# A decay-attention and snake-MLP kernel: head tables and casts placed anew, and the second and third chunks' scores and state products moved among the projection matmuls

## Chip, cores, metric

One core of one Trainium2 chip runs the whole program. The metric is device time of one launch in microseconds (us). The time before is the median of three runs, 211.49 us (210.94 to 211.74).

The engines are TensorE (PE; its weight loads are shown as PEld), VectorE (DVE), ScalarE (ACT), GpSimd (POOL) and SyncE (SP). Each runs its own instructions strictly in the order in which the program lists them, and waits on semaphores for what other engines and transfers deliver. So where an instruction stands in its engine's list decides what is queued behind it while it waits.

## What is computed

Attention with a decay per head over blocks, then an MLP with a snake activation:

```python
# q, k, v: [4, 8, 768, 64]; lam: [8], 0.97 to 0.99
for b in range(nb):                       # blocks along the sequence
    intra = einsum('bhic,bhjc->bhij', qb, kb) * Dmask     # lam**(i-j), i >= j
    intra = einsum('bhij,bhjd->bhid', intra, vb)
    inter = einsum('bhid,bhde->bhie', qb * lam_pow, kv_state)
    out = intra + inter
    kv_state = lam_block * kv_state + einsum('bhsd,bhse->bhde', kb * rev_pow, vb)
x = out.transpose(0, 2, 1, 3).reshape(3072, 512)
h = x @ w_in                              # [3072, 2048]
s = sin(alpha * h)
g = h + s * s / (alpha + 1e-9)
y = g @ w_out                             # [3072, 512], float32
```

## The kernel before

The sequence of 768 is cut into six chunks of 128 rows, t = 0 to 5. A chunk of all four batches gives 512 rows of x; the MLP on them is group g = t. While group g runs through the MLP, the attention of chunk g+1 is slotted between its matmuls. Nothing schedules this: the order of every engine is that in which the source emits it.

Attention of one chunk. k and q are turned (transposed) so that heads lie on partitions, by TensorE and a copy (`turn`, `turns_pair`) or by a transposing transfer (`turn_by_dma`). `scores` are the products of k and q. `masks` multiply them on VectorE with the decay mask. `states` are the products of decayed k (`kdec`, made by GpSimd in `decay_k`) and v. `update` adds them on VectorE to the decayed state and has GpSimd cast the new state (`cast_state`). `outputs_first` multiplies q with the state, `outputs` adds the masked scores times v in the same PSUM bank, and `leave` moves that with the row decay to `xt`, the MLP's input. Chunk 0 has no state yet and uses one block of 128: `scores1`, `outs`, `states1`, with the mask table C0. Its k and q are handled batch by batch; batch 0 and k of batch 1 come as float32 and are cast on VectorE. `spin` issues matmuls of no use that fill TensorE's time in the head.

MLP of one group. `hidden(g, f)` is four matmuls for one of 16 feature tiles f, a sine on ScalarE, and a square, on ScalarE or for some f of group 0 on VectorE (`squarer`). `finish` makes the gated value `gall` on VectorE from square, `r_sb` = 1/alpha and the PSUM bank. `project(g, m, part)` is four matmuls with a quarter of w_out (one unit); after part 3 `store` evicts the row m. Units of group g wait in a list, and `run(n)` takes the next n of it: most of group 0's between and after its own hidden tiles, the rest in group 1.

There are eight PSUM banks, named by number in the source. A bank is written again only when its last reader is done; the hidden tiles of group 0 go through `H0 = (0,1,2,3,5,6,7,4,0,1,3,5,0,1,5,0)`. GpSimd issues all loads after the first three (`load`, `load_w_in`, `load_w_out`), in its own order with its products. SyncE issues the transposing transfers and the stores.

The places that the change touches: the decay tables (L182 to 190); `squarer` (L442) and `store` (L485); the head, L516 to 565; the order after group 0's last hidden tile, L627 to 659; and the tables of what goes before and behind each f of group 1 (`slots`, `feed`, `own`, `units`, L662 to 707).

Of the kernel before, what the change touches and what calls it, by code (L numbers as in the profile page):

```python
# [8 lines left out]
ALU = mybir.AluOpType  # L9
# [6 lines left out]
def kernel(  # L16
# [11 lines left out]
    nc = tc.nc  # L28
# [153 lines left out]
    def decay_tables():  # L182
        nc.scalar.copy(out=lnlam[:, H:H + 2], in_=lnlam[:, 0:2])
        later["R128"] = powers("R128", 2, lnlam[:], [P, H + 2])
        later["NE64"] = powers("NE64", 3, lnlam[:].rearrange("p (hp hd) -> p hd hp", hd=2), [P, 2, HE])
        later["R64"] = powers("R64", 4, lnlam[:], [P, H + 2])
        for pr in range(2):
            for hd, half in enumerate(HALF):
                nc.scalar.activation(out=L64[half, pr, :], in_=lnlam[half, pr + hd:pr + hd + H - 1:2],
                                     func=ACTF.Exp, scale=float(D))  # L190
# [251 lines left out]
    def squarer(g, f):  # L442
        if g == 0:
            return V if f in (3, 5, 7, 9, 11) else A
        return A
# [39 lines left out]
    def store(g, m):  # L485
        o_sb = outp.tile([P, DM], FP32, name="o_sb")
        if g < NT - 2 and (g or m < 2):
            nc.vector.tensor_copy(out=o_sb[:], in_=ops_of.pop((g, m))[:])  # L488
        else:
            nc.scalar.copy(out=o_sb[:], in_=ops_of.pop((g, m))[:])  # L490
        held.append((m * S + g * T, o_sb))
        if g:
            put_held()
# [6 lines left out]
    def project_halves(g, m):  # L500
        for n in range(2):
            cols = slice(n * DM // 2, (n + 1) * DM // 2)
            ps = bank("hps", HB[n])
            for f in range(NFC):
# [13 lines left out]
                            in1=Rq[:].unsqueeze(2).broadcast_to([P, H, D]))  # L518
    nc.vector.tensor_copy(out=kn[0][:, 1, :, :], in_=raw["k1"][:])
    nc.vector.tensor_tensor(out=C0[:], in0=tri[:].unsqueeze(1).unsqueeze(1).broadcast_to([P, 2, HP, T]),  # L520
                            in1=NE[:].unsqueeze(3).broadcast_to([P, 2, HP, T]), op=ALU.mult)
    turn(0, "k", 0, 4, A)
    spin(2, 3)
    turn(0, "q", 0, 5, A)
    spin(2, 3)
    turn(0, "k", 1, 1, A)
    spin(3, 3)
    scores1(0, 0, (6, 7))
    turn(0, "q", 1, 2, A)
    spin(2, 3)  # L530
    nc.sync.dma_start(out=alpha_fp[:], in_=moe_alpha.rearrange("(f p) -> f p", p=P))
    turn(0, "k", 2, 0, A)
    spin(2, 3)
    scores1(0, 1, (4, 5))
    turn(0, "q", 2, 1, A)
    etab(0, 1)
    spin(3, 3)
    turn(0, "k", 3, 2, V)
    scores1(0, 2, (6, 7))
    spin(2, 3)  # L540
    turn(0, "q", 3, 0, A)
    etab(2, 3)
    decay_tables()
    spin(2, 3)
    a_ps = bank("a_ps", OB)
# [3 lines left out]
    nc.vector.tensor_copy(out=alpha_sb[:], in_=a_ps[:, 0:NFC])  # L549
    nc.vector.reciprocal(out=r_sb[:], in_=alpha_sb[:])  # L550
    spin(2, 1)
    scores1(0, 3, (4, 5))
    spin(2, 1)
    outs(0, 0, 3, A)
    outs(0, 1, 1)
# [4 lines left out]
    spin(3, 6)  # L560
    outs(0, 3, 0)
    spin(4, 6)
# [35 lines left out]
    for f in range(NFC):  # L598
        hidden(0, f)
        if f in (1, 10):  # L600
            states1(0, f // 10, 2 if f == 10 else 4)
        if f == 10:
            decay_k(1, 0, 2)
            decay_state(1, 0)
            cast_state(1, 0, home(1, 0))
            load_w_out(2)
            load(1, "q", 2, 4)
            load_w_out(3)
            load(2, "v", 0, 2)
        if f in (11, 12):  # L610
            run(1)
        if f == 12:
            turns_pair(1, "k", 0, 4, (A, A))
        if f == 13:
            turn(1, "q", 0, 2, A)
            turn(1, "q", 1, 3, V)
        if f == 14:
            scores(1, (0,), (4, 2))
            masks(1, 0)
        if f == 15:  # L620
            run(1)
            states(1, (0,), (3, 4))
            finish(0, 14)
            update(1, 0, 0)
        if f != 14:
            finish(0, f)
# [14 lines left out]
    run(3)  # L641
# [8 lines left out]
    run(1)  # L650
# [3 lines left out]
    run(1)  # L654
    outputs(1, (1,))
    leave(1, 1)
    run(1)
    decay_state(1, 0)
# [3 lines left out]
    def slots(g):  # L662
        t = g + 1
        d = {i: [] for i in range(NFC)}
        if g == 1:
            at = dict(KV=6, F=9, O=12)
        else:
            at = dict(KV=4, F=8, O=12)
        d[at["KV"]] += [(states, t)]
        for n in range(4):  # L670
            d[at["KV"] + ((0, 0, 1, 2)[n] if g == 1 else n)] += [(update, t, n // 2, n % 2)]
        d[at["F"]] += [(scores, t), (masks, t, 0)]
        d[at["F"] + 1] += [(masks, t, 1)]
        d[at["O"]] += [(outputs, t), (leave, t, 0)]
        d[at["O"] + (g > 1)] += [(leave, t, 1)]
        return d

    def feed(g):
        t = g + 1
        d = {i: [] for i in range(NFC)}  # L680
        if g == 1:
            d[2] += [(turn_by_dma, 2, 0, "k"), (pair_ready, 2, 1), (decay_state, 1, 1), (turn_by_dma, 2, 1, "k"), (turn_by_dma, 2, 0, "q")]
            d[7] += [(put_held,)]
            d[8] += [(turns_pair, 2, "q", 2, AB[0], (A, A))]
        if t + 1 < NT:
            if g == 1:
                d[7] += [(new_chunk, 3)] + [(load, 3, nm, b, b + 2) for nm, b in (("v", 0), ("k", 0), ("v", 2))]
                d[8] += [(load, 3, nm, b, b + 2) for nm, b in (("k", 2), ("q", 0), ("q", 2))]
# [10 lines left out]
    for g in range(1, NT + 1):  # L699
# [6 lines left out]
        own = {5: (0, 0), 8: (0, 1), 13: (0, 2)} if g == 1 else {}  # L706
        units = [1, 3, 5, 8, 13] if g == 1 else [i for i in range(NFC) if g > 2 or i not in (0, 1, 3)]
# [49 lines left out]
```

## Time and profile before

| | us |
|---|---|
| median of three runs | 211.49 |
| the profiled execution | 210.82 |
| its span on the core | 209.0 |
| TensorE busy | 201.0 |
| ScalarE busy | 143.1 |
| VectorE busy | 132.9 |
| GpSimd busy | 107.0 |

The span is the time from the first to the last instruction that the profiler saw; the difference to the execution's time lies around it. Busy time is what the profile shows of an engine's instructions. Matmuls are pipelined and overlap, so that TensorE's busy time is no measure of its rate. Single waits are read from the timeline, and which of them counts is read from the chain of waits, which follows the end of the program back from each step to what released it.

### The profile page before, as it was taken

How to read it: one execution, taken by the hardware profiler on the slowest of the kernel's cores; microseconds unless marked ns; L12 is line 12 of the kernel's file. 1: busy time of each engine (PE TensorE's matmuls, PEld its weight loads, DVE VectorE, ACT ScalarE, POOL GpSimd, SP SyncE). 2: the span in 40 equal slices, each digit the busy share in tenths (PEclk: the TensorE clock that was granted, in tenths of full speed). 3: DMA queues.
4: the chain of work that ended last, by engine and by line, in shares of the span. 5: the costliest groups of instructions: out<-in, count | busy, mean ns of one | idle time of the engine just before them, and what ended most of it. 6: DMA issues, size and time to landing. Idle time of an engine off the chain costs nothing.

```text
span 209.0 us, 5363 instructions
## 1 busy us (share of the span) xinstructions
PE 201.0 (96%) x2243; PEld 98.7 (47%) x2243; DVE 132.9 (64%) x218; ACT 143.1 (68%) x239; POOL 107.0 (51%) x111
## 2 busy tenths in 40 slices
PE   7999998999998999999999999999999999999993
PEld 2664444544453544445444444445444444444452
DVE  6794999473778868968547968556868544444000
ACT  4788989213999699765776775776675787887121
POOL 8989939979939993999986850002000000000000
PEclk9999999999999999999999999999999999999998
DMA  7999999999997999699999998701101101110212
GB/s 140 156 170 207 207 159 178 185 179 135 127 311 50 145 127 161 99 175 161 106 150 145 209 103 130 174 0 53 50 3 53 50 0 50 55 50 0 100 59 93
DMA packets 98794, 24.60 MB, mean 118 GB/s; under 512 B 90946, under 2 KB 95826, under 8 KB 98770
## 3 DMA queue, kind: packets, MB, share of 16 engines
q0 software_dynamic: 76176, 13.24, 86.7%
q1 hardware_dynamic: 20512, 10.50, 24.4%
q10 hardware_dynamic: 2082, 0.52, 1.4%
q8 instruction: 17, 0.28, 0.5%
q14 instruction: 7, 0.06, 0.1%
HBM read 27.27 MB, written 6.29 MB: 161 GB/s over the span
## 4 chain that ended last, share of the span: by engine, by line
PE 80%; DVE 11%; ACT 4%; DMA 2%; issue 1%; ACTq 0%
PE ops L481 37%; PE hps L453 33%; DVE gall L470 4%; DMA raw_k<-in_k_dram 2%; PE O_ps L403 2%; ACT s_sb L456 2%; ACT s L461 2%; PE hps L505 2%; DVE s L469 2%; DVE STm L304 2%; PE KV_ps L369 2%; PE O_ps L428 1%; PE F_ps L389 1%; DVE STm L396 1%; DVE xt L316 1%
## 5 line engine op out<-in xcount | busy, mean ns | idle before, releaser
L470 DVE SCALAR_TENSOR_TENSOR gall<-s,r_sb,hps 128x512 bf16<-128x512 bf16 x96 | 71.2, 745 | 45.0 <-ACT s L461 44.8
L453 PE MATMUL hps<-xt,w_in 128*128 128x512 bf16 x384 | 95.7, 379 | 1.2 <-DVE gall L470 0.5
L481 PE MATMUL ops<-w_out,gall 128*128 128x512 bf16 x368 | 92.4, 380 | 0.4 <-DVE gall L470 0.4
L456 ACT ACTIVATE s_sb<-hps,alpha_sb 128x512 bf16<-128x512 f32 x96 | 65.2, 684 | 32.1 <-PE hps L453 31.9
L461 ACT ACTIVATE s<-s_sb 128x512 bf16<-128x512 bf16 x91 | 57.3, 629 | 2.9
L453 PEld LDWEIGHTS <-w_in 128*128 128x128 bf16 x384 | 36.6, 98 | 44.1 <-issue 1.9
L481 PEld LDWEIGHTS <-gall 128*128 128x128 bf16 x368 | 34.6, 98 | 41.2 <-DVE gall L470 0.9
L236 POOL TENSOR_TENSOR kdec<-kn,R 128x1024 bf16<-128x1024 bf16 x12 | 22.8, 1924 | 3.2 <-DMA kn<-in_k_dram 3.2
L338 POOL CAST sb<-S 128x512 bf16<-128x512 f32 x20 | 12.3, 618 | 21.8 <-DVE S L345 20.6
L334 POOL TENSOR_TENSOR SD<-S,L 128x512 f32<-128x512 f32 x16 | 17.1, 1066 | 10.6 <-DVE S L345 10.5
L435 DVE TENSOR_TENSOR xt<-O_ps,Etab 128x512 bf16<-128x512 f32 x20 | 12.8, 685 | 6.3 <-PE O_ps L428 6.3
L104 POOL DMA_DIRECT2D vn<-in_v_dram x13 | 14.8, 1153 | 0.5 <-DMA w_in<-in_moe_w_in_dram 0.5
L396 DVE TENSOR_TENSOR STm<-F_ps,C 128x512 bf16<-128x512 f32 x20 | 12.8, 685 | 0.1
L488 DVE COPY o_sb<-ops 128x512 f32<-128x512 f32 x14 | 9.6, 689 | 4.2 <-PE ops L481 4.2
L490 ACT COPY o_sb<-ops 128x512 f32<-128x512 f32 x9 | 5.2, 577 | 9.7 <-PE ops L481 9.7
L345 DVE TENSOR_TENSOR S<-SD,KV_ps 128x512 f32<-128x512 f32 x16 | 10.8, 683 | 0.4 <-PE KV_ps L369 0.3
L128 PE MATMUL hps<-fill 128*128 128x256 bf16 (+1 forms) x40 | 9.7, 352 | 1.5 <-DVE fill L121 1.5
L277 ACT COPY QKT<-T_ps 128x512 bf16<-128x512 bf16 x9 | 5.2, 584 | 6.4 <-PE T_ps L275 6.4
L104 POOL DMA_DIRECT2D qn<-in_q_dram x8 | 8.8, 1099 | 0.3 <-issue 0.3
L104 POOL DMA_DIRECT2D kn<-in_k_dram x7 | 7.7, 1093 | 0.1
L403 PEld LDWEIGHTS <-sb 64*64 64x64 bf16 x320 | 4.3, 108 | 6.3 <-issue 6.3
L403 PE MATMUL O_ps<-QKT,sb 64*64 64x64 bf16 x320 | 5.9, 195 | 1.0 <-DVE STm L396 1.0
(75 smaller groups left out, 114.5 us busy)
## 6 DMA issues: line engine op xcount, KB each, us to landing
out_dram<-o_sb SPq DMA_DIRECT2D x23, 256.0 KB, 2.2
vn<-in_v_dram POOLq DMA_DIRECT2D x11, 256.0 KB, 7.5
w_out<-in_moe_w_out_dram POOLq DMA_DIRECT2D x4, 512.0 KB, 11.3
w_in<-in_moe_w_in_dram POOLq DMA_DIRECT2D x3, 512.0 KB, 11.6
kn<-in_k_dram POOLq DMA_DIRECT2D x5, 256.0 KB, 7.0
qn<-in_q_dram POOLq DMA_DIRECT2D x5, 256.0 KB, 9.9
kn<-in_k_dram POOLq DMA_DIRECT2D x5, 240.0 KB, 6.4
qn<-in_q_dram POOLq DMA_DIRECT2D x5, 240.0 KB, 9.0
```

Of the source, the lines that this page charges most:

```text
L104: nc.gpsimd.dma_start(out=to, in_=by_head)
L236: nc.gpsimd.tensor_tensor(out=kdec[t][:, b0:b1, :, :], in0=kn[t][:, b0:b1, :, :], in1=R[:, o:o + H].unsqueeze(1).unsqueeze(3).broadcast_to ...
L334: nc.gpsimd.tensor_tensor(out=pair(SD, pr), in0=pair(S_of[n], pr), op=ALU.mult, in1=L64[:, pr].unsqueeze(1).unsqueeze(3).broadcast_to([P, ...
L338: nc.gpsimd.tensor_copy(out=pair(dst, pr), in_=pair(S_of[n], pr))
L396: nc.vector.tensor_tensor(out=st[:, hd], in0=att["F", t, pr, hd], op=ALU.mult, in1=of_mask(C64, t, pr, hd).unsqueeze(1).broadcast_to([P, 2 ...
L403: nc.tensor.matmul(out=att["O", t, pr, blk][halves(h % 2), u, h // 2, :], lhsT=home(t, blk)[halves(half), 2 * pr + m // HP, m % HP, :], rh ...
L435: nc.vector.tensor_tensor(out=xview(t)[:, 2 * pr:2 * pr + 2, blk, :, :], in0=att["O", t, pr, blk], in1=Eb, op=ALU.mult)
L453: nc.tensor.matmul(out=hps[:], lhsT=w[:, c, (f % 4) * P:(f % 4 + 1) * P], rhs=xt[g][:, c, :], start=(c == 0), stop=(c == NDC - 1))
L456: nc.scalar.activation(out=s_sb[:], in_=hps[:], func=ACTF.Sin, scale=alpha_sb[:, f:f + 1])
L461: nc.scalar.activation(out=s2[:], in_=s_sb[:], func=ACTF.Square)
L470: nc.vector.scalar_tensor_tensor(out=gall[g][:, f, :], in0=s2[:], scalar=r_sb[:, f:f + 1], in1=hps[:], op0=ALU.mult, op1=ALU.add)
L481: nc.tensor.matmul(out=ops[:], lhsT=gall[g][:, f, m * P:(m + 1) * P], rhs=w_out_sb[part][:, f % 4, :], start=(f == 0), stop=(f == NFC - 1))
```

## The change

In the head: the mask table C0 is made in two halves around the cast of k1. The table copy and the exponential for R128 move ahead, the other exponentials behind the first outputs. One exponential E64 replaces the four small ones of L64, which are now copied out of it on VectorE. k of batch 3 is copied by ScalarE instead of VectorE. The alpha transposition and its copy (now on ScalarE) and the reciprocal move behind the first outputs. There are 33 useless matmuls instead of 40.

In group 0: f=1 is squared on VectorE and f=11 on ScalarE, the reverse of before. The last half of q of chunk 1 is loaded ahead of w_out2. Row m=2 is evicted by VectorE. Around the second half of chunk 1, one unit instead of three stands behind the state product, none between scores and first outputs, two before and two behind the outputs; one unit more is left for group 1.

In group 1: the state product of chunk 2 stands one f earlier, its scores before f=9 instead of behind it, and chunk 3's loads one f earlier. The units stand at f = 1, 3, 4, 8, 10, 13 (before: 1, 3, 5, 8, 13). The state decay of chunk 1's first half moves behind both `decay_k` of chunk 2.

```diff
-    def decay_tables():
-        nc.scalar.copy(out=lnlam[:, H:H + 2], in_=lnlam[:, 0:2])
+    E64 = consts.tile([P, H + 2], FP32, name="E64")
+    nc.scalar.copy(out=lnlam[:, H:H + 2], in_=lnlam[:, 0:2])
+
+    def decay_128():
         later["R128"] = powers("R128", 2, lnlam[:], [P, H + 2])
+
+    def decay_64():
         later["NE64"] = powers("NE64", 3, lnlam[:].rearrange("p (hp hd) -> p hd hp", hd=2), [P, 2, HE])
         later["R64"] = powers("R64", 4, lnlam[:], [P, H + 2])
+        nc.scalar.activation(out=E64[:], in_=lnlam[:], func=ACTF.Exp, scale=float(D))
+
+    def decay_of_pairs():
         for pr in range(2):
             for hd, half in enumerate(HALF):
-                nc.scalar.activation(out=L64[half, pr, :], in_=lnlam[half, pr + hd:pr + hd + H - 1:2],
-                                     func=ACTF.Exp, scale=float(D))
+                nc.vector.tensor_copy(out=L64[half, pr, :], in_=E64[half, pr + hd:pr + hd + H - 1:2])
...
-            return V if f in (3, 5, 7, 9, 11) else A
+            return V if f in (1, 3, 5, 7, 9) else A
...
-        if g < NT - 2 and (g or m < 2):
+        if g < NT - 2 and (g or m < 3):
...
+    def mask_128(hd):
+        nc.vector.tensor_tensor(out=C0[:, hd], in0=tri[:].unsqueeze(1).broadcast_to([P, HP, T]),
+                                in1=NE[:, hd].unsqueeze(2).broadcast_to([P, HP, T]), op=ALU.mult)
+
+    mask_128(0)
     nc.vector.tensor_copy(out=kn[0][:, 1, :, :], in_=raw["k1"][:])
-    nc.vector.tensor_tensor(out=C0[:], in0=tri[:].unsqueeze(1).unsqueeze(1).broadcast_to([P, 2, HP, T]),
-                            in1=NE[:].unsqueeze(3).broadcast_to([P, 2, HP, T]), op=ALU.mult)
+    mask_128(1)
     turn(0, "k", 0, 4, A)
     spin(2, 3)
     turn(0, "q", 0, 5, A)
+    decay_128()
     spin(2, 3)
     turn(0, "k", 1, 1, A)
-    spin(3, 3)
     scores1(0, 0, (6, 7))
     turn(0, "q", 1, 2, A)
-    spin(2, 3)
     nc.sync.dma_start(out=alpha_fp[:], in_=moe_alpha.rearrange("(f p) -> f p", p=P))
     turn(0, "k", 2, 0, A)
-    spin(2, 3)
+    spin(1, 3)
     scores1(0, 1, (4, 5))
     turn(0, "q", 2, 1, A)
-    etab(0, 1)
+    spin(1, 3)
+    turn(0, "k", 3, 2, A)
+    spin(1, 3)
+    scores1(0, 2, (6, 7))
+    turn(0, "q", 3, 0, A)
+    etab(0, 1, 2, 3)
     spin(3, 3)
-    turn(0, "k", 3, 2, V)
-    scores1(0, 2, (6, 7))
-    spin(2, 3)
-    turn(0, "q", 3, 0, A)
-    etab(2, 3)
-    decay_tables()
-    spin(2, 3)
-    a_ps = bank("a_ps", OB)
+    scores1(0, 3, (4, 5))
+    spin(3, 3)
+    outs(0, 0, 3, A)
+    decay_64()
+    outs(0, 1, 1)
+    a_ps = bank("a_ps", 7)
     nc.tensor.transpose(out=a_ps[:, 0:NFC], in_=alpha_fp[:], identity=idf[:])
...
-    nc.vector.tensor_copy(out=alpha_sb[:], in_=a_ps[:, 0:NFC])
-    nc.vector.reciprocal(out=r_sb[:], in_=alpha_sb[:])
-    spin(2, 1)
-    scores1(0, 3, (4, 5))
-    spin(2, 1)
-    outs(0, 0, 3, A)
-    outs(0, 1, 1)
+    nc.scalar.copy(out=alpha_sb[:], in_=a_ps[:, 0:NFC])
...
     outs(0, 2, 2)
-    spin(3, 6)
+    spin(4, 6)
     outs(0, 3, 0)
-    spin(4, 6)
+    spin(5, 6)
+    decay_of_pairs()
+    nc.vector.reciprocal(out=r_sb[:], in_=alpha_sb[:])
...
+            load(1, "q", 2, 4)
             load_w_out(2)
-            load(1, "q", 2, 4)
             load_w_out(3)
...
     update(1, 0, 1)
-    run(3)
+    run(1)
     turn(1, "q", 2, 5, A)
     turn(1, "q", 3, 0, V)
...
     load(2, "k", 2, 4)
-    run(1)
     outputs_first(1, (1,), (4, 2))
...
-    run(1)
+    run(2)
     outputs(1, (1,))
     leave(1, 1)
-    run(1)
-    decay_state(1, 0)
+    run(2)
     pair_ready(2, 0)
...
-            at = dict(KV=6, F=9, O=12)
+            at = dict(KV=5, F=9, O=12)
...
-        d[at["F"]] += [(scores, t), (masks, t, 0)]
-        d[at["F"] + 1] += [(masks, t, 1)]
+        if g > 1:
+            d[at["F"]] += [(scores, t), (masks, t, 0)]
+        d[at["F"] + (g > 1)] += [(masks, t, 1)]
...
-            d[2] += [(turn_by_dma, 2, 0, "k"), (pair_ready, 2, 1), (decay_state, 1, 1), (turn_by_dma, 2, 1, "k"), (turn_by_dma, 2, 0, "q")]
+            d[2] += [(turn_by_dma, 2, 0, "k"), (pair_ready, 2, 1), (decay_state, 1, 0), (decay_state, 1, 1), (turn_by_dma, 2, 1, "k"), (turn_by_dma, 2, 0, "q")]
...
+            d[9] += [(scores, 2), (masks, 2, 0)]
...
-                d[7] += [(new_chunk, 3)] + [(load, 3, nm, b, b + 2) for nm, b in (("v", 0), ("k", 0), ("v", 2))]
-                d[8] += [(load, 3, nm, b, b + 2) for nm, b in (("k", 2), ("q", 0), ("q", 2))]
+                d[6] += [(new_chunk, 3)] + [(load, 3, nm, b, b + 2) for nm, b in (("v", 0), ("k", 0), ("v", 2))]
+                d[7] += [(load, 3, nm, b, b + 2) for nm, b in (("k", 2), ("q", 0), ("q", 2))]
...
-        own = {5: (0, 0), 8: (0, 1), 13: (0, 2)} if g == 1 else {}
-        units = [1, 3, 5, 8, 13] if g == 1 else [i for i in range(NFC) if g > 2 or i not in (0, 1, 3)]
+        own = {8: (0, 0), 10: (0, 1), 13: (0, 2)} if g == 1 else {}
+        units = [1, 3, 4, 8, 10, 13] if g == 1 else [i for i in range(NFC) if g > 2 or i not in (0, 1, 3)]
```

## The prediction

> **What bounds the kernel now.** I read the page first, then TensorE's timeline, then the chain of waits, then the landing of single transfers. In the timelines each row gives start and length in us, engine, line, operation, count, and in brackets the idle time before it and who ended it.
>
> ```profile
> span 209.0 us, 5363 instructions
> PE 201.0 (96%) x2243; PEld 98.7 (47%) x2243; DVE 132.9 (64%) x218; ACT 143.1 (68%) x239; POOL 107.0 (51%) x111
> PE 80%; DVE 11%; ACT 4%; DMA 2%; issue 1%; ACTq 0%
> w_out<-in_moe_w_out_dram POOLq DMA_DIRECT2D x4, 512.0 KB, 11.3
> ```
>
> TensorE is busy for 96% of the span and carries 80% of the chain that ended last. No useful matmul is removed, so only its waiting can be won, and 201.0 of 209.0 us leaves 8 us at most. The timeline says where it lies.
>
> ```profile
> 1.45 1.89 PE L128 MATMUL hps<-fill 128*128 128x512 bf16 x4 [1.45 <-DVE fill L121]
> ...
> 12.11 0.23 PE L546 MATMUL a_ps<-idf,alpha_fp 16*128 16x16 f32 x1
> ...
> 16.32 1.89 PE L453 MATMUL hps<-xt,w_in 128*128 128x512 bf16 x8 [0.34 <-DVE xt L316]
> ...
> 27.70 1.04 PE L481 MATMUL ops<-w_out,gall 128*128 128x512 bf16 x4
> ...
> 32.69 1.02 PE L453 MATMUL hps<-xt,w_in 128*128 128x512 bf16 x4 [0.47 <-DVE gall L470]
> 33.79 0.45 PE L389 MATMUL F_ps<-QKT 64*64 64x64 bf16 x32
> ...
> 45.81 0.45 PE L389 MATMUL F_ps<-QKT 64*64 64x64 bf16 x32
> ...
> 47.16 0.69 PE L403 MATMUL O_ps<-QKT,sb 64*64 64x64 bf16 x31
> ...
> 50.61 1.89 PE L453 MATMUL hps<-xt,w_in 128*128 128x512 bf16 x8 [0.43 <-DVE xt L435]
> ...
> 60.01 1.04 PE L453 MATMUL hps<-xt,w_in 128*128 128x512 bf16 x4
> 60.88 0.61 PE L289 MATMUL T_ps<-iden,qn 128*128 128x128 bf16 x8
> ...
> 62.19 0.81 PE L481 MATMUL ops<-w_out,gall 128*128 128x512 bf16 x3
> 63.39 0.39 PE L481 MATMUL ops<-w_out,gall 128*128 128x512 bf16 x1 [0.39 <-DVE gall L470]
> ...
> 67.93 0.22 PE L403 MATMUL O_ps<-QKT,sb 64*64 64x64 bf16 x3 [0.64 <-DVE STm L396]
> 68.53 0.66 PE L403 MATMUL O_ps<-QKT,sb 64*64 64x64 bf16 x59 [0.38 <-DVE STm L396]
> 69.12 1.04 PE L453 MATMUL hps<-xt,w_in 128*128 128x512 bf16 x4
> ```
>
> I call four matmuls of L453 (one feature tile f) a hidden block, hf, and four of L481 a unit. A block ends 1.03 us after its start, but the next starts 0.865 after it (two rows in sequence: 60.01 and 60.88). So an idle time after a block costs itself and 0.17 more: 0.43 before 50.61 costs 0.60, 0.39 before 63.39 costs 0.56. The two waits inside the 64 small matmuls at 67.07 to 69.12 cost nearly their whole steps, 0.85 and 0.57. From 69.12 on no such wait follows: what is won before 69.12 at an equal number of blocks shortens the span one for one.
>
> **Part 1, the head up to 16.32 (C0 in halves, k3 by ScalarE, tables moved, 33 fills for 40).** I cost it at nothing, because two transfers pin what follows.
>
> ```profile
> L92 POOL DMA_DIRECT2D w_out<-in_moe_w_out_dram x1: 745/745/745, 13.2 to 13.2; - x1
> ...
> DMA to landing us min/median/max: 14.5/14.5/14.5
> ```
>
> The first w_out piece is issued at 13.2 and lands 14.5 later, at 27.7; the first unit starts at 27.70. Its place in GpSimd's queue isn't changed, so whatever h0 gains, TensorE waits there until 27.7. Hence the head can't gain, only lose: h0 later than 16.32 passes on. The alpha transposition now stands between the first chunk's outputs with one more fill; by its row that is 0.23, and a 256-column fill is half of the 0.216 step of a 512 one, 0.11. Against it, seven fills are gone ahead of them. I take 0, bounds 0 and +0.35.
>
> ScalarE's four exponentials for L64 become one (E64), which with the copy of k3 and alpha is about even; its sine table is loaded behind them and is wanted only when h0 has ended. The four small copies and the reciprocal go to VectorE behind its last product before h0, beside GpSimd's products. Such company can be dear:
>
> ```profile
> 29.67 1.90 POOL L236 TENSOR_TENSOR kdec<-kn,R 128x1024 bf16<-128x1024 bf16 x1 [3.18 <-DMA kn<-in_k_dram]
> ...
> 29.72 2.13 DVE L469 TENSOR_TENSOR s<-s_sb 128x512 bf16<-128x512 bf16 x1
> ```
>
> f=11's square ended at 31.85, 0.28 after GpSimd's product. If two of the five small instructions wait like that, the first gall product is 3.8 us late at most. What covers it: the bank of f=0 is needed again by h8 only, eight blocks, 6.9 us, after h0, when ScalarE's own work for f=0 has taken some 2 of them; a product and a square per pair then still keep pace. Cost 0; with that cover gone it would be what exceeds about 4 us.
>
> **Part 2, squares of f=1 and f=11 swapped between the engines.** The wait of 0.47 at h14 falls: its bank is freed by f=11's product, which stood behind the 2.13 us square. But the stall goes to the next late thing.
>
> ```profile
> 29.64 0.69 ACT L456 ACTIVATE s_sb<-hps,alpha_sb 128x512 bf16<-128x512 f32 x1 [0.60 <-PE hps L453]
> ```
>
> h12 follows the first unit (27.70 + 0.865) and ends 1.03 later, 29.6: there ScalarE starts, with two sines, two squares and three copies ahead of the scores at 33.79. Sine and square take 1.26, a copy 0.53 (both below): 2 x 1.26 + 3 x 0.53 = 4.1, 29.64 to 33.75. All of it stays. So TensorE idles ahead of the scores instead of ahead of h14. f=11's square on ScalarE fits into its 0.60 of idle time, since f=1's is gone. Gain 0, bounds 0 and 0.6.
>
> **Part 3, second chunk's last scores and outputs adjacent (33.79 to 50.61).** Until the second state product nothing moves. Then three units become one, and the unit between scores and outputs goes behind them; a unit with w_out2 runs just ahead of the scores.
>
> ```profile
> 42.84 0.68 DVE L345 TENSOR_TENSOR S<-SD,KV_ps 128x512 f32<-128x512 f32 x1
> ...
> 45.06 0.42 DVE L279 COPY QKT<-T_ps 128x512 bf16<-128x512 bf16 x1 [1.54 <-PE T_ps L275]
> 45.40 1.11 DVE L349 SCALAR_TENSOR_TENSOR S<-S,L,KV_ps 128x128 f32<-128x128 f32 x4
> ```
>
> With three units fewer in front, the first outputs would start at 47.16 - 3 x 0.865 = 44.57. They write the bank that VectorE's L349 reads. VectorE is free at 43.5 (42.84 + 0.68), and copy and L349 take 1.45 (45.06 to 46.51): 44.95. That is a new wait of 0.4, with the two units queued behind it. The wait of 0.60 before h0 goes: two units, 1.73, now cover two VectorE evictions of 0.68. One unit is carried into the next group: h0 = 50.61 - 0.60 - 0.865 + 0.4 = 49.55. At equal work 0.2 is gained. Bounds: -0.4, if VectorE comes one instruction of 0.68 later, and +0.6, if the new wait is nothing.
>
> The second half of q is now loaded ahead of w_out2:
>
> ```profile
> L92 POOL DMA_DIRECT2D w_out<-in_moe_w_out_dram x1: 823/823/823, 33.3 to 33.3; - x1
> ...
> DMA to landing us min/median/max: 8.0/8.0/8.0
> ```
> ```profile
> L101 POOL DMA_DIRECT2D qn<-in_q_dram x1: 1204/1204/1204, 34.1 to 34.1; - x1
> ...
> DMA to landing us min/median/max: 9.0/9.0/9.0
> ```
>
> w_out2 landed at 41.3, q behind it at 43.1. Exchanged, the later of the two should land at that same 43.1, now w_out2. Its first unit stands one unit and the scores (0.38, 45.81 to the next unit) before 44.57, so at 43.3. It just fits. q comes earlier, as the turns, two units earlier, need.
>
> **Part 4, third chunk in group 1.** State product one block earlier, scores before h9 instead of behind it, a unit more between scores and outputs. h0 to h8 with their pieces keep their lengths, so I add the distances of before to 49.55. h6 now ends behind the state product: 49.55 + (60.01 - 50.61) = 58.95, and 0.17: 59.12. From there ScalarE sets the pace:
>
> ```profile
> 61.08 0.69 ACT s_sb L456
> ...
> 61.80 0.61 ACT s L461
> ...
> 62.80 0.59 ACT QKT L292
> 63.39 0.60 ACT s_sb L456
> ...
> 64.01 0.64 ACT s L461
> ...
> 64.67 0.75 DVE gall L470
> 65.42 1.20 DVE STm L396 x2
> ...
> 67.27 1.21 DVE STm L396 x2
> ```
>
> A sine with its square takes 1.26 (63.39 to 64.65), and with two copies 2.31 (61.08 to 63.39). So: sine 6 at 59.15, sine 7 at 60.41, then copies, sine 8 at 62.72, its product on VectorE at 62.72 + 1.28 = 64.0, the masks at 64.75, all four in sequence 2.4: 67.15. TensorE: turns at 49.55 + 10.27 = 59.82, h8 and unit to 59.82 + 1.31 + 0.87 = 62.0, scores held by the copies until 62.7, then h9, h10, unit, h11 (3.46) to about 66.5. It waits for the masks until 67.15 again, and 0.64 later (68.48 to 69.12) h12 starts: 67.8, with as many units done as before. 69.12 - 67.8 = 1.3, of which 0.2 is part 3 and 1.1 this part. Bounds of this part: 0.5, if VectorE's chain comes one 0.68 later, and 1.98, if its three waits vanish.
>
> **Smaller moves.** The state decay of chunk 1 now stands in GpSimd's queue behind chunk 2's two products (1.90 each, as at 29.67). The update that reads it comes after the state product, which needs both of them in any case: 0, and one GpSimd instruction if that cover is gone. Chunk 3's loads are issued a block earlier behind that update, and the m=2 row of group 0 leaves by VectorE (0.68, as its evictions) between products that wait for ScalarE: 0.
>
> **Sum.** 0 + 0 + 0.2 + 1.1 = 1.3. The profiled execution has span 209.0 and 210.82 around it: span 207.7, 209.5. The median of the runs is 211.49, 0.67 higher than the profiled one; on it 210.2.
>
> **Rivals.**
> First, a wait takes the place of the removed ones. Part 3 at its lower bound, -0.4, and part 4 near its own, 0.6: 0.2, so 211.3. For it: ScalarE and VectorE ended every wait quoted above, and none of their work disappears there. Against it: part 3's own count, which gives back 0.4 of 0.60.
>
> Second, all waits quoted vanish: 0.6 + 1.98 = 2.6, 208.9. ScalarE's count above speaks against it.
>
> Third, slower: w_out2 behind q. The unit at 43.3 waits for it, and all TensorE work behind. It is issued 1.8 us later than before (33.3 to 35.1). With its own 8.0 it lands at 43.1. With the median of its four, 11.3, at 46.4: 3.1 of wait, less the 1.3, 213.3. It eats the whole gain from a landing at 44.6 on, 9.5 after its issue. For it: the other loads of this weight took up to 14.5. Against it: the transfers queued ahead of it are the same bytes as before.
>
> Fourth, the thinner fills let TensorE's clock fall. The rows at 1.45 and 16.32 show both rates: four matmuls of 512 columns in 1.89, later eight. The slow stretch at the start lasts about 4 us (two such rows and what lies between, to 5.5). Starting at h0 it would cost half of that, 2.0, passed on at 27.70: 2.0 - 1.3 = +0.7, 212.2. Against it: seven fills of 0.11 are 0.8 us, spread over the 10 from 5.5 to 16.32. The Trainium skill, "TensorE: Matmul & The Clock Gate", section "What's actually happening", has the half rate return after at least one idle window of about 3.4 us; by that the head stays fast, and no run here shows such a fall. That keeps this rival small.
>
> **How the numbers follow.** Forecast 0.60, first rival 0.17, second 0.07, third 0.09, fourth 0.07. The forecast's own range is 0.7 to 1.9 gained, 209.6 to 210.8. 0.5%, 1.06 us, is about what a measurement of this kernel can tell from no change: faster means under 210.43. Of the forecast 0.45 lies there and 0.15 within; with the second rival faster is 0.52; within 0.5% are 0.15, the first rival and 0.05 of the fourth, 0.37; slower the third and the rest, 0.11. The range 209.1 to 212.3 leaves out the second and third rivals, 0.16.
>
> **What would show it.** Right: h0 of group 0 wherever it likes near 16.3, but the first unit at 27.7 and the first scores of group 0 at 33.8; a wait of about 0.4 before the outputs at 45; h0 of group 1 at 49.5 without a wait; h12 at 67.8 behind a mask wait of about half a us. Wrong: a first unit that moves with the head (then the transfers pinned nothing), a wait on w_out near 43.3, a hidden block whose matmuls stand 0.43 apart, or an h12 later than 69.1.

## The result, and the profile after

| | before | after |
|---|---|---|
| median of five runs, us | 211.11 | 210.09 |
| lowest and highest, us | 210.83, 211.74 | 209.95, 210.19 |
| the profiled execution, us | 210.82 | 210.19 |
| its span, us | 209.0 | 208.4 |

The changed kernel takes 0.9941 of the time before, 95% interval 0.9923 to 0.9959: 1.02 us less at the medians. The forecast was 1.3 less and 210.2. The before of these runs lay at 211.11, not at the 211.49 on which the forecast stood, and the gain was 0.3 smaller; the two nearly cancel in the time.

The page of the changed kernel first: span, busy time, and the granted TensorE clock in 40 slices.

```profile
span 208.4 us, 5325 instructions
PE 197.9 (95%) x2206; PEld 98.3 (47%) x2236; DVE 135.6 (65%) x222; ACT 142.5 (68%) x237; POOL 106.9 (51%) x111
PEclk9999999999999999999999999999999999999999
```

No engine's share has moved by more than a point, and the clock stays full: the gain is in single waits. They stand in TensorE's timeline of the changed kernel (start and length in us, engine, line, operation, count, idle time before and who ended it; the lines named here are 6 higher than before):

```profile
16.61 1.89 PE L459 MATMUL hps<-xt,w_in 128*128 128x512 bf16 x7 [0.23 <-DVE xt L322]
...
28.18 1.04 PE L487 MATMUL ops<-w_out,gall 128*128 128x512 bf16 x4
29.29 1.02 PE L459 MATMUL hps<-xt,w_in 128*128 128x512 bf16 x4
...
34.51 0.45 PE L395 MATMUL F_ps<-QKT 64*64 64x64 bf16 x32 [0.71 <-ACT QKT L283]
...
43.40 0.68 PE L281 MATMUL T_ps<-iden,qn 128*128 128x128 bf16 x8
43.91 1.03 PE L487 MATMUL ops<-w_out,gall 128*128 128x512 bf16 x4
...
45.65 0.66 PE L409 MATMUL O_ps<-QKT,sb 64*64 64x64 bf16 x30 [0.31 <-DVE S L355]
...
50.21 1.89 PE L459 MATMUL hps<-xt,w_in 128*128 128x512 bf16 x7
...
63.42 0.73 PE L395 MATMUL F_ps<-QKT 64*64 64x64 bf16 x64 [0.60 <-ACT QKT L298]
64.31 1.67 PE L459 MATMUL hps<-xt,w_in 128*128 128x512 bf16 x7 [0.16 <-issue]
...
67.64 0.87 PE L409 MATMUL O_ps<-QKT,sb 64*64 64x64 bf16 x63
68.50 1.02 PE L459 MATMUL hps<-xt,w_in 128*128 128x512 bf16 x3
```

Five points of this timeline cut the program into stretches: the first unit, the first scores of chunk 1, h0 of group 1, h12 of group 1, the end. From the rows above and those that the prediction shows of before:

| stretch, us | before | after | gain at equal work |
|---|---|---|---|
| to the first unit | 27.70 | 28.18 | -0.48 |
| to chunk 1's first scores | 6.09 | 6.33 | -0.24 |
| to h0 of group 1 | 16.82 | 15.70 | 0.26 (one unit of 0.865 is carried on) |
| to h12 of group 1 | 18.51 | 18.29 | 1.09 (that unit is done here) |
| to the end | 139.89 | 139.88 | 0.01 |

So parts 3 and 4 brought 0.26 and 1.09, 1.35 in all, and 0.72 was given back in front of them. Of that, 0.29 was there at h0 of group 0 already (16.61 for 16.32). That it comes from the change is not shown: in the profiles here h0 moves by more than that under one and the same head, with the old head from 16.32 to 17.14, with the new one and all its fills from 16.45 to 17.03. Of these, the two late ones, of the runs x_part4 and x_both below, are those in which k of batch 1 landed latest, at 7.28 and 7.30 (before: 6.92). The other 0.43 arises between h0 and the scores. The unit at 28.18 waits for the transfer, h12 at 29.29 for a VectorE product. VectorE's timeline shows why the product is late:

```profile
16.38 4.01 DVE L196 COPY L<-E 64x4 f32<-64x4 f32 x4
20.42 0.26 DVE L570 RECIPROCAL r_sb<-alpha_sb 128x16 f32<-128x16 f32 x1
20.79 0.75 DVE L476 SCALAR_TENSOR_TENSOR gall<-s,r_sb,hps 128x512 bf16<-128x512 bf16 x1
...
24.28 1.41 DVE L476 SCALAR_TENSOR_TENSOR gall<-s,r_sb,hps 128x512 bf16<-128x512 bf16 x2
25.60 0.42 DVE L475 TENSOR_TENSOR s<-s_sb 128x512 bf16<-128x512 bf16 x1
26.06 1.41 DVE L476 SCALAR_TENSOR_TENSOR gall<-s,r_sb,hps 128x512 bf16<-128x512 bf16 x2
27.38 0.42 DVE L475 TENSOR_TENSOR s<-s_sb 128x512 bf16<-128x512 bf16 x1
27.84 1.41 DVE L476 SCALAR_TENSOR_TENSOR gall<-s,r_sb,hps 128x512 bf16<-128x512 bf16 x2
```

L64's four tiny copies take 4.01 us, and the first gall product starts at 20.79 (before: 18.76). No row from there to 33 us has idle time in front. Two products and a square repeat every 1.78 us (24.28 to 26.06 to 27.84), and TensorE makes two hidden blocks in 1.73. So VectorE can't catch up, and h12 at 29.29 waits for the last product of the last row, which frees its bank. The chain that ended last, followed through this stretch, says the same:

```profile
16.46 2.65 DVE L L196
...
19.30 0.91 DVE L L196
...
27.84 1.42 DVE gall L476 x2
...
29.29 1.04 PE hps L459 x4
```

The first copy was held for 2.65 us, the third for 0.91. GpSimd's timeline shows what ran beside them:

```profile
14.10 3.77 POOL L242 TENSOR_TENSOR kdec<-kn,R 128x1024 bf16<-128x1024 bf16 x2
17.82 1.26 POOL L205 TENSOR_TENSOR C<-tri,NE 128x640 f32<-128x640 f32 x1
19.03 1.22 POOL L104 DMA_DIRECT2D kn<-in_k_dram  x1
```

The first copy ends at 19.11, right after the mask table's product (17.82 + 1.26 = 19.08). The third ends at 20.21, with the first load's issue (19.03 + 1.22 = 20.25).

The transfer of w_out0, by its line in that window:

```profile
L92 POOL DMA_DIRECT2D w_out<-in_moe_w_out_dram x1: 747/747/747, 13.3 to 13.3; - x1
...
DMA to landing us min/median/max: 14.8/14.8/14.8
```

It was issued 0.2 later than before and took 0.3 longer. In the eleven profiles here that leave its place alone it landed between 27.53 and 28.53. It holds TensorE only a little: in the five profiles at a full clock in which w_out0 is there 0.3 us or more before its unit, the unit stands 11.31 or 11.32 behind h0 (x_part4, x_l64act, x_wout0, x_both, x_early4 below). In the kernel before it stood 11.38 behind, here 11.57. So the transfer held the unit by 0.06 before and by 0.25 here.

### The profile page after: what moved, and what is told of

It reads as the page before. It is cut to its first block, busy times and chain, and to the rows that moved or that the text cites. A ratio compares the mean times of both kernels' runs of the same rounds, so it can differ in the third digit from the quotient of the medians.

```text
span 208.4 us, 5325 instructions
## 1 busy us (share of the span) xinstructions
PE 197.9 (95%) x2206; PEld 98.3 (47%) x2236; DVE 135.6 (65%) x222; ACT 142.5 (68%) x237; POOL 106.9 (51%) x111
## 4 chain that ended last, share of the span: by engine, by line
PE 80%; DVE 8%; ACT 4%; DMA 3%; issue 2%; POOL 2%; POOLq 0%; DVEq 0%; ACTq 0%
PE ops L487 36%; PE hps L459 33%; DVE gall L476 3%; DMA qn<-in_q_dram 3%; PE O_ps L409 2%; DVE L L196 2%; PE hps L511 2%; PE F_ps L395 2%; PE KV_ps L375 1%; PE O_ps L434 1%; ACT s_sb L462 1%; POOL qn L104 1%; POOL kn L104 1%; ACT s L467 1%; ACT QKT L298 1%
## 5 line engine op out<-in xcount | busy, mean ns | idle before, releaser
L459 PE MATMUL hps<-xt,w_in 128*128 128x512 bf16 x369 | 94.2, 379 | 1.4 <-issue 0.3
L487 PE MATMUL ops<-w_out,gall 128*128 128x512 bf16 x353 | 90.3, 379 | 1.0 <-issue 0.3
L494 DVE COPY o_sb<-ops 128x512 f32<-128x512 f32 x15 | 10.3, 689 | 4.2 <-PE ops L487 4.1
L496 ACT COPY o_sb<-ops 128x512 f32<-128x512 f32 x8 | 4.6, 577 | 12.0 <-PE ops L487 12.0
L128 PE MATMUL hps<-fill 128*128 128x256 bf16 (+1 forms) x33 | 8.2, 359 | 1.5 <-DVE fill L121 1.5
L283 ACT COPY QKT<-T_ps 128x512 bf16<-128x512 bf16 x10 | 5.7, 585 | 4.3 <-PE T_ps L281 4.2
L104 POOL DMA_DIRECT2D kn<-in_k_dram x7 | 7.6, 1087 | 0.0
L101 POOL DMA_DIRECT2D kn<-in_k_dram x5 | 6.2, 1235 | 0.0
```

Of the source, the lines that this page charges most:

```text
L104: nc.gpsimd.dma_start(out=to, in_=by_head)
L459: nc.tensor.matmul(out=hps[:], lhsT=w[:, c, (f % 4) * P:(f % 4 + 1) * P], rhs=xt[g][:, c, :], start=(c == 0), stop=(c == NDC - 1))
L487: nc.tensor.matmul(out=ops[:], lhsT=gall[g][:, f, m * P:(m + 1) * P], rhs=w_out_sb[part][:, f % 4, :], start=(f == 0), stop=(f == NFC - 1))
```

## The experiments

Every ratio is to the kernel before on the same chip. Interval: 95%.

**One part alone.** Four kernels, each the kernel before with one part of the change, in the same five rounds; its median there was 211.03.

x_head has the whole head part; of the change these edits, and all behind the head, are undone:

```diff
-            return V if f in (1, 3, 5, 7, 9) else A
+            return V if f in (3, 5, 7, 9, 11) else A
...
-        if g < NT - 2 and (g or m < 3):
+        if g < NT - 2 and (g or m < 2):
```

> The kernel before with the head of the changed one alone (C0 in halves, tables, alpha, k3 by ScalarE, fewer fills, L64 copied by VectorE); squares, loads and units as before. Pinning theory: the landing of the first w_out piece sets the first unit whatever the head does, so 0 (within 0.3 us of before), first unit within 0.1 of that landing. VectorE's small copies wait for GpSimd (about 4 us in the changed kernel) and could add up to 0.3 at h12. Rival, the head is a source of the gain: 0.5 us or more faster.

Measured: 210.99 against 211.03, ratio 1.0 (0.9988 to 1.0012). The first unit stands at 27.89, its w_out landed at 27.85, and h14 waits 0.49 as before: the next distance is 6.10. The head alone is worth nothing.

x_square:

```diff
-            return V if f in (3, 5, 7, 9, 11) else A
+            return V if f in (1, 3, 5, 7, 9) else A
```

> The kernel before with the squares of f=1 and f=11 swapped alone. Theory: the wait of 0.47 before h14 goes and comes back as 0.6 to 0.8 before the first scores of chunk 1, ended by ScalarE's copy; 0 (within 0.3 us). Rival, the 2.13 us square was a cost of its own: 0.5 us faster.

Measured: 211.08, ratio 1.0001 (0.9989 to 1.0014). TensorE's timeline of this kernel, around the scores:

```profile
32.44 1.03 PE L453 MATMUL hps<-xt,w_in 128*128 128x512 bf16 x4
34.18 0.44 PE L389 MATMUL F_ps<-QKT 64*64 64x64 bf16 x32 [0.71 <-ACT QKT L277]
```

The wait before h14 is gone, and 0.71 stands before the scores instead. The distance from first unit (28.09) to scores is 6.09, as before. The stall moved and cost what it had cost.

x_part3:

```diff
-    run(3)
+    run(1)
...
     load(2, "k", 2, 4)
-    run(1)
     outputs_first(1, (1,), (4, 2))
...
-    run(1)
+    run(2)
     outputs(1, (1,))
     leave(1, 1)
-    run(1)
+    run(2)
```

with the new order of the loads, the new place of the state decay, row m=2 by VectorE, and the carried unit behind f = 4.

> The kernel before with part 3 alone: units around the second half of chunk 1, q ahead of w_out2, m=2 by VectorE, the state decay behind both products; group 1 as before with one unit more at f=4. Theory: 0.2 us faster (bounds 0.6 faster, 0.4 slower), no wait before h0 of group 1, a new one of 0.3 to 0.4 in the first outputs. Rival, this part carries the gain: 0.8 us or more faster.

Measured: 211.01, ratio 1.0007 (0.9984 to 1.003), 210.54 to 212.76. The stretch to h0 of group 1 is 15.70 here too, 0.26 gained, and h0 waits for nothing. But the last stretch is 140.35 long, 0.46 more than before. TensorE's timeline of this kernel has a wait there that neither before nor after has:

```profile
117.98 0.45 PE L389 MATMUL F_ps<-QKT 64*64 64x64 bf16 x32
118.68 0.45 PE L389 MATMUL F_ps<-QKT 64*64 64x64 bf16 x32 [0.26 <-DMA QKT<-qn]
```

The scores of chunk 4 wait there for the transposing transfer of its q, so the 0.26 doesn't show at the end of this execution. The medians don't show it either: part 3 alone can't be told from no change by its time.

x_part4 has the four edits of `slots`, `feed`, `own` and `units` for group 1, and the new place of the state decay:

```diff
-            at = dict(KV=6, F=9, O=12)
+            at = dict(KV=5, F=9, O=12)
...
+            d[9] += [(scores, 2), (masks, 2, 0)]
...
-        own = {5: (0, 0), 8: (0, 1), 13: (0, 2)} if g == 1 else {}
-        units = [1, 3, 5, 8, 13] if g == 1 else ...
+        own = {8: (0, 0), 10: (0, 1), 13: (0, 2)} if g == 1 else {}
+        units = [1, 3, 8, 10, 13] if g == 1 else ...
```

> The kernel before with part 4 alone: state product of chunk 2 behind f=5, scores before f=9, a unit at f=10 instead of f=5, chunk 3's loads one f earlier, the state decay behind both products; chunk 1 as before. Theory: 1.1 us faster (bounds 0.5 and 2.0), the three waits between 62 and 69 us replaced by one before the scores. Rival, it works only with the earlier h0 of part 3: under 0.4 faster.

Measured: 209.96, ratio 0.9946 (0.9926 to 0.9966). TensorE's timeline of this kernel:

```profile
51.35 1.02 PE L453 MATMUL hps<-xt,w_in 128*128 128x512 bf16 x4 [0.43 <-DVE xt L435]
...
67.91 0.87 PE L403 MATMUL O_ps<-QKT,sb 64*64 64x64 bf16 x63
68.77 1.02 PE L453 MATMUL hps<-xt,w_in 128*128 128x512 bf16 x4
```

h0 to h12 takes 68.77 - 51.35 = 17.42 rather than 18.51: 1.09, the same as within the whole change. Both mask waits are gone; a wait of 0.17 for ScalarE's copies stands before the scores. This part alone brings as much as the whole change.

**What was given back.** Four kernels on the changed one, whose own median is 210.09. A pin, in what was expected, is what sets a point of the timeline whatever is won ahead of it.

x_l64act:

```diff
-                nc.vector.tensor_copy(out=L64[half, pr, :], in_=E64[half, pr + hd:pr + hd + H - 1:2])
+                nc.scalar.copy(out=L64[half, pr, :], in_=E64[half, pr + hd:pr + hd + H - 1:2])
```

> The changed kernel with L64's four copies on ScalarE instead of VectorE (they fall in its idle time before the first sine). Theory: VectorE's first product comes some 1.5 us or more earlier than 20.8, the wait of h12 on VectorE (0.24) goes, the scores of chunk 1 come as much earlier: 0.2 us faster than the changed kernel, 0.1 to 0.4. Rival, VectorE's delay is fully covered: no wait moves, 0.

Measured: 209.9, ratio 0.9938 (0.9912 to 0.9963). That median is 0.19 under the changed kernel's, as expected, but within the intervals. Eight of its twelve executions took 209.49 to 210.06, the other four 210.85 to 211.09; three of these four have a mean clock of 0.992, the others 0.998 or more. Its timelines, ScalarE's and then VectorE's:

```profile
16.23 0.80 ACT L196 COPY L<-E 64x4 f32<-64x4 f32 x4
```

```profile
19.07 0.75 DVE L476 SCALAR_TENSOR_TENSOR gall<-s,r_sb,hps 128x512 bf16<-128x512 bf16 x1 [2.49 <-ACT s L467]
```

Four copies cost 0.80 on ScalarE, inside its idle time, and the first product is 1.72 earlier. The first unit is at 27.88, the scores at 33.96, 6.08 apart: the wait at h12 is gone. The profiled execution is one of the four long ones, with the late wait of x_part3, now longer:

```profile
116.93 0.44 PE L395 MATMUL F_ps<-QKT 64*64 64x64 bf16 x32
118.39 0.44 PE L395 MATMUL F_ps<-QKT 64*64 64x64 bf16 x32 [1.02 <-DMA QKT<-qn]
```

x_wout0 issues w_out0 ahead of the last piece of w_in:

```diff
-    for i in range(1, 4):
+    for i in range(1, 3):
         load_w_in(i)
+    load_w_out(0)
+    load_w_in(3)
```

> The changed kernel with the first w_out piece loaded ahead of the last w_in piece. Pinning theory: that piece lands some 2.5 us earlier, the first unit follows its hidden block without a wait, and 0.2 to 0.3 us are gained until the next pin (last w_in piece at h12, VectorE at h12). Rival, nothing pinned there: 0, the first unit at its time.

Measured: 210.04, ratio 0.9943 (0.9923 to 0.9962). w_out0 lands at 25.13. TensorE's timeline of this kernel:

```profile
27.77 1.03 PE L489 MATMUL ops<-w_out,gall 128*128 128x512 bf16 x4
29.14 1.02 PE L461 MATMUL hps<-xt,w_in 128*128 128x512 bf16 x4 [0.35 <-DVE gall L478]
```

The unit doesn't wait any more, and h12 waits longer for the same product. The scores start at 34.36, in the changed kernel at 34.51. So VectorE was the pin behind h0, and the later landing merely lay in front of it. Counted from h0 this is plain: with copies and square on VectorE the scores start 17.90 or 17.91 behind h0, whether w_out0 is late (the changed kernel), in time (x_qlate, where h12 waits 0.34) or far ahead (here). With the copies on ScalarE they start 17.40 behind it in x_l64act and 17.39 in x_both, before 17.47.

x_both has both edits.

> The changed kernel with both edits: L64 by ScalarE and the first w_out piece ahead of the last w_in piece. Theory: the two waits lie one behind the other on TensorE, so both go only together: 0.4 to 0.6 us faster than the changed kernel, if the last w_in piece is there for h12. Rival: ScalarE's chain to the scores begins no earlier, 0.

Measured: 209.65, ratio 0.9923 (0.9898 to 0.9948), 209.42 to 210.08: the lowest median of all kernels here, 0.44 under the changed kernel, though that was measured in other executions and the two intervals overlap. In its profile k of batch 1 landed late (7.30), the first unit stands at 28.34 behind a later head, and still nothing waits at h12.

x_qlate puts the load of q behind w_out2 again:

```diff
-            load(1, "q", 2, 4)
             load_w_out(2)
+            load(1, "q", 2, 4)
             load_w_out(3)
```

> The changed kernel with the load of chunk 1's second half of q behind w_out2 again, as before the change; all else as changed. Theory (part 3 needs the new load order, since its turns of q stand two units earlier): before the change q landed at 43.1 with w_out2 ahead of it; shifted by the 0.48 of the later first unit, 43.6. In the changed kernel TensorE comes to the turns at 43.40, so it waits 0.2 to 0.3 for q there, and all behind it ends 0.2 to 0.3 later: h0 of group 1 some 16.0 us after the first scores of group 0 rather than 15.70, in all about 0.2 over the changed kernel, near 210.3. Third rival's view (w_out2 behind q is the danger, and the landing in the changed kernel, 43.4 for a use at 43.9, is just in time): with w_out2 first again nothing waits, and the distance stays 15.70. Bad landings of q (up to 1.2 us late, as other loads show) would give 1 us more in some executions.

Measured: 210.08, ratio 0.9954 (0.9937 to 0.997). My theory falls: the stretch is 15.70 again. Line 101 of this kernel, the load of q, in its window:

```profile
L101 POOL DMA_DIRECT2D qn<-in_q_dram x1: 1204/1204/1204, 34.1 to 34.1; - x1
...
DMA to landing us min/median/max: 8.8/8.8/8.8
```

q landed at 42.87 (its last 16 KB at 43.03) for turns at 43.35, and w_out2 at 41.31. In the changed kernel q landed at 40.60, and w_out2 at 43.42 for its unit at 43.91. Either order just fits; the exchange brought nothing.

**The late wait.** Its guess was a late load of q, so chunk 4's loads go two hidden blocks earlier, in x_both and in x_part3:

```diff
-                a = 6 if g == 2 else 2
+                a = 4 if g == 2 else 2
```

> The version with L64's copies on ScalarE and w_out0 ahead of the last w_in, and with one more edit: chunk 4's loads are issued two hidden blocks earlier in group 2 (f = 4 and 6 for 6 and 8). Its own theory: in x_l64act, x_part3 the scores of chunk 4 near 118 us waited 1.02 and 0.26 us for the transposing transfer of chunk 4's q, because its load landed late; with the loads about 3.5 us earlier that wait is gone in every execution, so the upper of the two values of x_l64act (210.9 to 211.1) does not occur, and the time is that of the former version, 209.4 to 210.1, median 209.65. Rival: the wait is set by something else (the queue of SP, the stores), the upper value occurs again in some executions. Second rival: the earlier loads meet the stores of group 1 and move a wait to 80 to 95 us; the time is 0.3 or more above 209.65.

> The kernel before with part 3 alone, and chunk 4's loads two hidden blocks earlier. Theory: part 3 is worth 0.26 us at h0 of group 1 and lost it only to the late transfer near 118 us; without that wait it comes out 0.2 to 0.3 below the kernel before, ratio near 0.9988, and no wait for the transfer near 118. Rival: part 3 is worth nothing at the end of the program whatever happens at 118 (the gain is lost at another place): ratio 1.000.

Measured: 213.84, ratio 1.0108 (1.0067 to 1.0148), and 213.44, 1.0125 (1.0084 to 1.0165). On the time both guesses fall; x_early4's second rival was right in place, with a price far above its least of 0.3. TensorE's timelines, x_early4 and then x_part3_early4:

```profile
88.76 0.45 PE L397 MATMUL F_ps<-QKT 64*64 64x64 bf16 x32 [2.27 <-DMA QKT<-qn]
```

```profile
90.40 0.45 PE L389 MATMUL F_ps<-QKT 64*64 64x64 bf16 x32 [2.78 <-DMA QKT<-qn]
```

Now chunk 3's scores wait. In x_early4 the first three of chunk 4's loads were issued from 77.0 to 80.5, and the transposing transfer of chunk 3's q in the middle of them. By its line, in x_early4 and then in x_both:

```profile
L260 SPq DMA_TRANSPOSE QKT<-qn x1: 1287/1287/1287, 79.2 to 79.2; - x1
...
DMA to landing us min/median/max: 9.4/9.4/9.4
```

```profile
L260 SPq DMA_TRANSPOSE QKT<-qn x2: 1231/1232/1232, 78.0 to 79.4; - x2
...
DMA to landing us min/median/max: 4.3/4.6/4.9
```

Issued at the same time, it takes 9.4 us beside those loads and 4.3 to 4.9 without them.

The guess on the wait near 118 us is borne out all the same. Chunk 4's scores come in one piece in both profiles (119.29 and 122.60) and wait for nothing. Before each transposing transfer of q SyncE waits for its load. By the line of these transfers, near 105 us, in x_part3 and then in x_part3_early4:

```profile
L252 SPq EVENT_SEMAPHORE  x1: 2152/2152/2152, 105.7 to 105.7; - x1
```

```profile
L252 SPq EVENT_SEMAPHORE  x2: 17/22/28, 105.1 to 110.3; - x2
```

In x_part3 the second half of chunk 4's q landed at 107.84; SyncE stood 2.15 us, issued the transfer at 108.7, and it landed at 118.55. In x_l64act SyncE stood 3.48 us there (q landed at 108.18), and the transfer landed at 118.25. In the ten other profiles with these loads in the old place SyncE stood there 1.21 us at most and issued by 107.8, and no scores near 118 us wait. With the earlier loads SyncE doesn't stand there; the transfer landed at 118.70 in x_part3_early4, 3.9 us ahead of its scores. So the late load made the wait, and moving the loads cost more than the wait. What makes the load late in some executions stays open.

**No fills.** x_nofill is the changed kernel without the 25 small fills that follow the first turns; x_nofill2 is the same kernel again.

```diff
-    spin(2, 3)
...
-    spin(3, 6)
...
-    spin(4, 6)
...
-    spin(5, 6)
```

> The changed kernel with all 25 fills of 256 columns between the head's matmuls taken out. Transfers set the head: h0 within 0.3 us of its place and the time within 0.4 us. Clock rival: matmuls of the first group 0.43 us apart instead of 0.216 for some microseconds, 1 to 2 us slower.

> The same kernel as x_nofill (the changed kernel without its 25 head fills after the first products), for a second profile. Of ten executions of x_nofill four had a mean granted clock of 0.975 to 0.984 and 211.9 to 212.2 us; its profile was of one with 0.999 and 210.9. Theory (the fourth rival's mechanism, when all fills go): where the clock falls, it falls in the head or just behind it, the matmuls of that stretch take twice their 0.22 us, and the head ends later; such a profile shows the granted clock below 1.00 in one or several slices before 40 us and steps of 1.73 for 0.865 there. Rival: the clock falls at another place (behind the wait near 118 us), or the 212.2 us executions with clock 1.00 show that a transfer does it and the clock costs nothing.

Measured: 212.13, ratio 1.0027 (0.9999 to 1.0054), and 211.99, 1.0036 (1.0008 to 1.0064). These are 2.0 and 1.9 over the changed kernel, so the theory of x_nofill, a time within 0.4, falls. The profile of x_nofill shows a full clock (210.89), that of x_nofill2 (211.94) a fallen one. Its windows of some 3.4 us (busy time and instructions of each engine; then granted clock, DMA share, GB/s):

```profile
5.94:9.36 3.42, 2.05 (x30) 1.36 (x30) 3.20 (x6) 2.77 (x7) 3.42 (x4) 0.98 2.36 155
9.36:12.78 3.42, 2.71 (x28) 1.77 (x25) 2.58 (x5) 1.98 (x5) 3.18 (x5) 0.50 2.66 154
12.78:16.20 3.42, 2.81 (x41) 2.17 (x40) 2.88 (x6) 3.31 (x11) 2.93 (x3) 0.50 1.67 189
16.20:19.60 3.40, 2.64 (x7) 1.02 (x8) 3.37 (x4) 1.40 (x4) 3.40 (x3) 0.52 1.24 207
19.60:23.00 3.40, 3.40 (x31) 1.62 (x30) 3.21 (x7) 2.71 (x5) 3.40 (x4) 1.00 1.24 206
```

The clock is halved from 9.25 to 19.5 us. The first unit comes at 29.39, 1.21 behind that of the changed kernel, and the first scores at 35.48, 0.97 behind. The rest of the 1.75 by which this execution is longer doesn't come from the halved clock: from the scores to h0 of group 1 the program takes 16.53 instead of 15.70, at a full clock. TensorE stands 0.65 us there, at 47.64, amid the outputs, for nothing that the profile shows. x_nofill's profile has 0.26 of the same, at 46.64. Of the 20 executions of this kernel seven had a mean clock of 0.967 to 0.984 and took 211.9 to 212.7. But seven more took 212.0 to 214.2 at a clock of 0.999 or 1.00, the rest 210.7 to 211.3; what held those seven isn't shown. One execution took 295.21 at a mean clock of 0.678, which no theory here covers.

## Why the prediction came out right, and where its steps were off

- Part 1, the head: cost 0. Alone it is 0 (x_head, 210.99 against 211.03). Within the change it isn't: of the 0.72 given back, 0.43 arises behind h0, and there VectorE's lateness is the pin. The failed step is "What covers it: the bank of f=0 is needed again by h8 only". That looked at one bank, with the wait between the first product and its next use. "a product and a square per pair then still keep pace" holds only nearly, and to keep pace is not to make up lost time: at 1.78 us for a pair of products against TensorE's 1.73 for the pair of blocks VectorE can't, and its lateness, 2.03 at the first product, holds up h12. The delay itself was within its bound (3.8 at most).
- "TensorE waits there until 27.7" was a near tie. At the pace of 11.32 from h0 TensorE would have come to the first unit at 27.64, so the transfer held it by 0.06. The prediction's own sign of being wrong, a first unit that moves with the head, is there in part: in x_both h0 is at 17.03 and the first unit at 28.34, with w_out0 landed at 25.58. That the head alone gains nothing holds (x_head).
- It takes both zero-cost parts. x_head has the 4.01 us of copies as well, and x_square the swapped square; neither makes h12 wait, x_head by a mere 0.05 (its product ends at 28.72, h12 starts at 28.77). Only the two together do, because f=1's square now stands on VectorE in just the stretch in which it is late.
- Part 2, the squares: 0, with the stall moved from h14 to the scores. Right, with 0.71 there in x_square and in the changed kernel.
- Part 3: 0.2, with a new wait of 0.4 and h0 without one. Measured: 0.26 by the stretch of the timeline, the new wait 0.31, h0 at 50.21; less the 0.72 it came with, 49.49 for the forecast 49.55. The step on the loads ("q comes earlier, as the turns, two units earlier, need") failed: x_qlate does without, if only by 0.3 us.
- Part 4: 1.1. Measured 1.09, alone and within the change. h12 at 68.50 is 67.78 less the 0.72, forecast 67.8, and ScalarE's copies do hold the scores (63.42 less 0.72 is 62.70, forecast 62.7). But the mask wait forecast behind them didn't come. From 62.7 the blocks and the unit (3.46) lead to 66.16; "about 66.5" left 0.34 for the scores, which took 0.89 (63.42 to 64.31). So TensorE comes to the outputs at 66.92 (67.64 less the 0.72), when the masks are all but done: VectorE ends the last at 67.80, which is 67.08, forecast 67.15. The outputs start at once, 0.23 ahead of the forecast, and take 0.86 to h12 rather than 0.64. The two errors cancel in h12, so that its place is right by luck.
- First rival (a wait takes the place): 0.72 of the 1.35 was given back, 0.43 of it by waits, but in front of the parts that it named, not in them. Second rival: two of the waits it would have had vanish are there, 0.31 and 0.60. Third: w_out2 landed at 43.42 and its unit started at 43.91; no wait, 0.5 us from one. Fourth: with 33 fills the clock stays full in every execution of the changed kernel; without 25 of them the mechanism is there, at about half the price that was written (0.97 at the first scores; forecast 2.0). The prediction's sentence that no run shows such a fall holds for the runs it had.
- The sum: 1.3 forecast, 1.35 found in parts 3 and 4, 0.72 given back in the profiled execution and some 0.3 at the medians. Without the 0.29 that stood at h0 already the profiled execution gives 1.35 - 0.43 = 0.92, near the 1.02 of the medians. That the measured 210.09 lies so near the forecast 210.2 is partly luck: the kernel before came out 0.38 lower, and the gain 0.28 smaller.

## What to carry to other kernels

An instruction moved to an engine "with slack" costs nothing only if that engine later has idle time in which to make up the delay; compare its period per tile with that of the engine it feeds, not only the next use of one buffer. A moved load is tried against the transfers of other chunks that are in flight when it is issued: two blocks earlier cost 2.4 and 4.2 us here, at the medians. And where several edits go in together, the part-alone runs show which of them is the change: here one of four.

## What the runs showed of the hardware

- Copies of 64 x 4 float32 values from SBUF to SBUF took 4.01 us for four on VectorE beside GpSimd's products and load issues, 0.80 on ScalarE. The Trainium skill, "SBUF — State Buffer", section "Who interferes with whom", has a copy on VectorE, in the modes in which it uses the port pair that it shares with GpSimd, and a GpSimd instruction lock each other out for the length of the first; no view here shows the mode of a copy. The trace agrees for the third copy, though the second ran 0.17 us long while the same load issue was under way (19.12 to 19.29); the first stayed locked out beyond the instruction it met, until the next product behind it had ended too (16.46 to 19.11).
- TensorE's clock falls to half in steps: in x_nofill2 9.25 to 19.5 us is three times 3.42, and after the 2.78 us wait at 90.40 in x_part3_early4 the clock is at half from 91.3 to 94.6; the mean clock lacks 0.008 of 213.6, 1.7 us, which is one such step at half. The Trainium skill, "TensorE: Matmul & The Clock Gate", section "What's actually happening", has free-running windows of about 3.4 us, of which one idle one halves the rate; the lengths agree. But TensorE was busy for 2.05 of the 3.42 us before the fall at 9.25, so that such a window need not be idle; in x_nofill's profile, busy for 1.88 of them, the clock stayed full. The same program shows the fall in some executions and not in others.
- A transposing transfer took 4.3 to 4.9 us from issue to landing in x_both (3.7 and 4.0 in the changed kernel), and 9.4 when the loads of another chunk were issued around it (chunk 3's q at 78 to 80 us). Chunk 4's two of q, in the kernel before issued at 104.0 and 106.2 while chunk 5's loads go out, took 8.9 and 10.0.
